# Attention over a KV cache, two blocks: VectorE's copy of the overflow flag ahead of or behind the last sum

## The chip, the cores and the metric

The kernel runs on one core of a Trainium2 chip. The core has five engines, each with its own instruction stream: TensorE (PE, matmuls; PEld are its weight loads), VectorE (DVE), ScalarE (ACT), GpSimd (POOL) and SyncE (SP, which here issues nearly all DMAs). They meet only at semaphores. The metric is the device time of one execution in microseconds (us), lower is better. Before the change it is 738.27 us, the median of three runs (737.86, 738.27 and 738.68).

A profiled execution gives a trace. Its times are counted from the first instruction of the program; the time from there to the last instruction is called the span.

## What is computed

Two independent attention blocks, A and B, with the same shapes. Their results stand side by side in the output.

```python
B, Sq, D = 16, 64, 640
H, Sk, Dh = 32, 512, 128

def block(x, k_cache, v_cache, wq, wo):
    q = (x @ wq).reshape(B, Sq, H, Dh).transpose(0, 2, 1, 3)
    scores = einsum("bhqd,bhkd->bhqk", q, k_cache) * Dh ** -0.5
    o = einsum("bhqk,bhkd->bhqd", softmax(scores), v_cache)
    return o.transpose(0, 2, 1, 3).reshape(B, Sq, H * Dh) @ wo

out = concatenate([block(A...), block(B...)], axis=-1)      # 16 x 64 x 1280, bfloat16
```

All inputs are bfloat16. The two key and two value caches are by far the most of what is read.

## The kernel before

**Tiles and stages.** Two batch entries are handled together, so that 2 x 64 query rows fill 128 partitions. A *pack* is such a pair of batch entries with four heads; there are 128 packs. For each pack the kernel projects the queries (QP), transposes the keys on VectorE (KT), computes the scores (S), takes the exponential on ScalarE (EX), multiplies by the reciprocal of the row sum on GpSimd (NM), transposes the probabilities (TR, copied out by TE), multiplies by the values (PV, copied out by OE) and adds the product with the output weights to PSUM (OP). Four packs make a group, and after a group VectorE adds its part to an accumulator (OS). When the last heads of a block are in, SP stores 128 rows of the output (ST).

**The order of the work.** It is written out by hand. `build_plan` gives every operation a time, in units of packs, from the table `AT` in `Cfg`, and each engine executes its operations sorted by that time. From what each operation reads and writes, the semaphore waits are derived (`order_waits`): a wait that an earlier one on the same engine already covers is dropped. So to change a number in `AT` can change the place of an operation in its engine's order, and the waits with it.

**The exponential is taken without subtracting the maximum.** This holds as long as no row sum is out of bounds. Whether that was so is examined at the end: VectorE reduces all reciprocals to a maximum and a minimum and makes a 0 or 1 for each of 128 partitions (FL1, lines 907 to 916), TensorE multiplies that vector with itself to the number of good partitions (FLM, a matmul of one element, line 919), and VectorE copies the number to SBUF as an integer (FLC, line 923). This integer is the flag. Every engine, at the end of its program, waits for the flag copy, loads the flag into a register (line 987) and branches (line 988): at 128 over the general version of the program, which is in the code but not executed here, and otherwise into it. SP then waits until the output has landed:

```python
def run(e, eng):
    run_program(e, eng, 0)
    e.wait_ge(sems[0][("s_flc_dve",)], 1)
    ...
        e.reg_load(r, flag[0:1, 0:1])
        e.br_eq(r, 128, on_true=over, on_false=again).branch_hint(ahead[eng])
    ...
    if eng == "sp":
        all_done(e, 0, ("d_out",))
```

**The last pack** is done in finer steps, so that the end is short. Its product with the output weights is made in two halves of 320 columns (OPH, line 827), VectorE adds each half to the accumulator (OSH, line 835: the sums of the change), and SP stores each half as soon as its sum is there (STH, line 842). In the table `AT` the first sum stands at 1.75, the flag copy at 1.77 and the second sum at 1.8; the stores stand at 1.85 and 1.9, on SP. On TensorE the flag's matmul (1.68) stands between the matmuls of the first half (1.65) and the second (1.7). Line 529 is that of the block that holds all five programs: to it the trace puts SP's wait for the output and the drains and semaphores that close the program.

Of the kernel before, what the change touches and what calls it, by code (L numbers as in the profile page):

```python
# [20 lines left out]
class Cfg:  # L21
# [16 lines left out]
              RCZ=(0.475, 0.6), NMZ=(0.48, 0.49, 0.61, 0.62), TR=1.293, TE=(1.432, 1.47), PV=1.701, OE=(1.888, 2.013), ZO=2.221,  # L38
              OP=2.387, OS=2.576, LDWO=2.6, ST=2.8,
              TRH=(1.0, 1.05), TEH=(1.15, 1.2), TEX=1.2, PVH=(1.45, 1.46), OEH=(1.5, 1.55), OPY=(1.1, 1.57),  # L40
              OPZ=(1.65, 1.7), OSH=(1.75, 1.8), STH=(1.85, 1.9), FL1=1.3, FLM=1.68, FLC=1.77, WP0=-1.75,
              WP1=(-3.5, -2.55, -2.45, -1.5, -0.5, 0.5, 0.6, 1.5))


# [42 lines left out]
def build_plan(dims, cfg, general):  # L87
# [12 lines left out]
    def add(eng, kind, idx, ts, reads=(), writes=()):  # L100
        op = Op(eng, kind, idx, ts, reads, writes)
        ops.append(op)
        at[(kind, idx)] = op
        return op

    def add_output(n):
# [6 lines left out]
        if n == N - 1:  # L113
            for a in range(2):
# [5 lines left out]
                    [("B", 4), ("B", 5), ("xe", 0)] if a == 0 else [("SB", 2), ("SB", 3), ("xe", 1)])  # L120
                add("pe", "OPH", (n, a), n + AT["OPZ"][a], [("xe", 0), ("xe", 1), ("wo", j)], [("B", 6 + a)])
                add("dve", "OSH", (g, a), n + AT["OSH"][a], [("acc", g % NBP)], [("B", 6 + a), ("out_sb", a)])
# [944 lines left out]
```

## Time and profile before

| | |
|---|---|
| median of three runs | 738.27 us (737.86 to 738.68) |
| the profiled execution's own time | 737.86 us |
| its span, first to last instruction | 736.1 us |
| granted TensorE clock, mean | 0.981 of full speed |
| busy share of the span: PE / PEld / DVE / ACT / POOL | 92% / 72% / 72% / 72% / 57% |
| DMA, mean over the span | 401 GB/s, 295 MB |

Times of the trace are microseconds from the start of the span unless they are marked ns. A line of the timeline has the start, the duration, the engine, the source line, the operation with what it writes and reads, and in brackets how long the engine was idle before and what ended that. The lower-case q behind an engine (SPq, PEldq) is its sequencer: there stand register loads, branches, semaphores and DMA issues, which do not count as busy. "DMA to landing" is the time from a DMA's issue to its last semaphore count. Where DMA packets are listed by queue, q1 carries the kernel's loads and stores, and q8 and q14 carry instructions, that is, program code. Shares of a DMA queue are shares of 16 DMA engines over the stretch asked for.

### The profile page before, as it was taken

How to read it: one execution, taken by the hardware profiler on the slowest of the kernel's cores; microseconds unless marked ns; L12 is line 12 of the kernel's file. 1: busy time of each engine (PE TensorE's matmuls, PEld its weight loads, DVE VectorE, ACT ScalarE, POOL GpSimd, SP SyncE). 2: the span in 40 equal slices, each digit the busy share in tenths (PEclk: the TensorE clock that was granted, in tenths of full speed). 3: DMA queues.
4: the chain of work that ended last, by engine and by line, in shares of the span. 5: the costliest groups of instructions: out<-in, count | busy, mean ns of one | idle time of the engine just before them, and what ended most of it. 6: DMA issues, size and time to landing. Idle time of an engine off the chain costs nothing.

```text
span 736.1 us, 61429 instructions
## 1 busy us (share of the span) xinstructions
PE 679.2 (92%) x28502; PEld 532.5 (72%) x28502; DVE 526.9 (72%) x819; ACT 533.2 (72%) x1574; POOL 416.5 (57%) x596
## 2 busy tenths in 40 slices
PE   3679999999989999999988999999998899999997
PEld 2457877877767777777766787777776678778785
DVE  7347877878767876867756777776676578788884
ACT  1348787877876887777865777777776687878874
POOL 3635656557864555454865565565577456555561
PEclk9889999999999999999998999999999999999999
DMA  8999999999999999999999999999999999999991
GB/s 325 393 392 411 415 415 414 414 416 413 416 400 410 417 417 416 415 419 416 416 412 400 416 414 414 414 414 413 416 416 405 404 418 417 415 419 416 417 400 45
DMA packets 76131, 295.06 MB, mean 401 GB/s; under 512 B 9536, under 2 KB 24512, under 8 KB 59712
## 3 DMA queue, kind: packets, MB, share of 16 engines
q1 hardware_dynamic: 73328, 291.90, 98.4%
q10 hardware_dynamic: 2768, 2.79, 1.2%
q8 instruction: 10, 0.16, 0.1%
q14 instruction: 25, 0.20, 0.1%
HBM read 292.03 MB, written 2.62 MB: 400 GB/s over the span
## 4 chain that ended last, share of the span: by engine, by line
PE 60%; DMA 27%; SPq 5%; DVE 3%; issue 2%; POOL 1%; ACT 0%; ACTq 0%
PE ps L863 14%; PE ps L883 13%; PE ps L684 12%; PE ps L708 12%; DMA wo_sb<-in_B_wo_dram 8%; PE ps L770 7%; DMA kn_ring<-in_B_k_cache_dram 5%; DMA kn_ring<-in_A_k_cache_dram 5%; DMA xn_ring<-in_B_x_dram 5%; SPq L631 3%; SPq L642 2%; DMA ws_sb<-in_A_wq_dram 2%; DMA wo_sb<-in_A_wo_dram 2%; DVE kt_ring L698 1%; DVE pT_sb L850 1%
## 5 line engine op out<-in xcount | busy, mean ns | idle before, releaser
L758 POOL TENSOR_SCALAR pn_ring<-pn_ring,recip 128x512 bf16<-128x512 bf16 x508 | 342.1, 692 | 244.9 <-DVE recip L750 238.5
L698 DVE STREAM_TRANSPOSE kt_ring<-kn_ring 128x1024 f32<-128x1024 f32 x256 | 302.4, 1220 | 65.9 <-DMA kn_ring<-in_B_k_cache_dram 35.7
L737 ACT ACTIVATE pn_ring<-ps 128x512 bf16<-128x512 f32 x512 | 296.4, 592 | 6.8 <-PE ps L708 6.8
L850 DVE COPY pT_sb<-ps 128x1024 bf16<-128x1024 bf16 x256 | 170.3, 676 | 103.5 <-PE ps L770 80.1
L863 PE MATMUL ps<-pT_sb,v_ring 32*128 32x64 bf16 x16448 | 162.1, 193 | 25.3 <-DVE pT_sb L850 12.7
L863 PEld LDWEIGHTS ps<-pT_sb,v_ring 32*128 32x128 bf16 x16448 | 147.5, 92 | 39.2 <-issue 28.7
L684 PE MATMUL ps<-xT_ring,wqp_sb 128*128 128x128 bf16 x2560 | 166.3, 221 | 7.5 <-POOL xT_ring L673 7.5
L684 PEld LDWEIGHTS ps<-xT_ring,wqp_sb 128*128 128x128 bf16 x2560 | 158.0, 114 | 14.0 <-issue 7.8
L883 PE MATMUL ps<-wo_sb,oT_sb 128*128 128x320 bf16 x1024 | 165.3, 305 | 0.0
L871 ACT ACTIVATE oT_sb<-ps 128x256 bf16<-128x256 f32 x257 | 84.7, 381 | 109.3 <-PE ps L863 109.3
L708 PE MATMUL ps<-kt_ring,qs_ring 32*64 32x512 bf16 x4096 | 140.6, 386 | 3.6 <-issue 3.6
L690 ACT ACTIVATE qs_ring<-ps 128x512 bf16<-128x512 f32 x128 | 76.4, 597 | 65.3 <-PE ps L684 62.6
L883 PEld LDWEIGHTS ps<-wo_sb,oT_sb 128*128 128x128 bf16 x1024 | 91.0, 99 | 37.9
L770 PEld LDWEIGHTS ps<-ident,pn_ring 64*128 64x128 bf16 x4096 | 68.8, 96 | 66.9 <-ACT oT_sb L871 48.0
L737 ACT ACTIVATION_READ_ACCUMULATOR pn_ring<-ps 128x1 f32 x512 | 105.3, 206 | 0.0
L770 PE MATMUL ps<-ident,pn_ring 64*128 64x64 bf16 x4096 | 83.8, 192 | 12.3 <-POOL pn_ring L758 4.5
L708 PEld LDWEIGHTS ps<-kt_ring,qs_ring 32*64 32x64 bf16 x4096 | 53.2, 104 | 33.2 <-issue 5.9
L750 DVE RECIPROCAL recip<-rowsum 128x2 f32<-128x2 f32 x256 | 41.0, 160 | 30.3 <-ACT pn_ring L737 24.6
L875 ACT ACTIVATE ps<-zeros 128x256 f32<-128x256 bf16 x128 | 49.5, 387 | 4.1
L652 POOL COPY wqp_sb<-ws_sb 128x1280 bf16<-128x1280 bf16 x32 | 39.5, 1253 | 18.3 <-DMA ws_sb<-in_A_wq_dram 15.1
L664 ACT ACTIVATE xe_sb<-ps 128x640 bf16<-128x640 bf16 x32 | 23.0, 717 | 3.6 <-PE ps L658 3.6
L673 POOL COPY xT_ring<-xe_sb 128x640 bf16<-128x640 bf16 x16 | 11.5, 716 | 21.9 <-PE ps L770 21.9
(42 smaller groups left out, 103.7 us busy)
## 6 DMA issues: line engine op xcount, KB each, us to landing
v_ring<-in_A_v_cache_dram SPq DMA_DIRECT2D x128, 512.0 KB, 12.9
kn_ring<-in_B_k_cache_dram SPq DMA_DIRECT2D x128, 512.0 KB, 14.0
v_ring<-in_B_v_cache_dram SPq DMA_DIRECT2D x128, 512.0 KB, 12.8
kn_ring<-in_A_k_cache_dram SPq DMA_DIRECT2D x112, 512.0 KB, 14.1
kn_ring<-in_A_k_cache_dram SPq DMA_DIRECT2D x32, 256.0 KB, 9.0
wo_sb<-in_A_wo_dram SPq DMA_DIRECT2D x8, 640.0 KB, 14.6
ws_sb<-in_B_wq_dram SPq DMA_DIRECT2D x10, 512.0 KB, 17.3
wo_sb<-in_B_wo_dram SPq DMA_DIRECT2D x8, 640.0 KB, 15.0
```

Source lines behind the costliest of these rows:

```text
L684: last = e.matmul(ps[:, 1, f * 128:(f + 1) * 128], w[:, kt, f, :], xT_ring[:, xs, kt, :], start=(kt == 0), stop=(kt == KT - 1))
L690: ins = e.activation(qs_ring[:, op.idx % NQ].rearrange("p f b q -> p (f b q)"), ps[:, 1, :], ACTF.Copy, scale=scale)
L698: ins = e.transpose(dst.rearrange("p c b (h l) -> p c h b l", h=8, l=2), src)
L708: last = e.matmul(ps[64 * b:64 * b + 64, i, :], qs_ring[rows, n % NQ, f, b, :], kt_ring[rows, n % NKT, :, f // 2, b, :, f % 2], start=(f = ...
L737: ins = e.activation(dst, src, ACTF.Exp, scale=1.0, accum_out=sum_of(h))
L758: ins = e.tensor_scalar(pn_view(h), pn_view(h), recip[:, h:h + 1], 1.0, ALU.mult, ALU.mult)
L770: last = e.transpose(pt_bank(b)[:, 64 * c:64 * c + 64], pn[rows, c, :], ident[rows, rows], tile_position=(64 * b, 0))
L850: ins = e.tensor_copy(pT_sb[:, b].rearrange("p t q -> p (t q)"), pt_bank(b))
L863: last = e.matmul(ps[:, 4 + i, 64 * b:64 * b + 64], v_ring[rows, n % NV, b, c, :], pT_sb[rows, b, c, :], start=(t == 0 and i < 2), stop=(t ...
L871: ins = e.activation(oT_sb[:, 2 * a:2 * a + 2, :], o_ps[:, 2 * a:2 * a + 2, :], ACTF.Copy)
L875: ins = e.activation(z_ps, zeros[:, :].unsqueeze(2).broadcast_to([128, 2, 128]), ACTF.Copy)
L883: last = e.matmul(out_ps[:, s, :], oT_sb[:, i, :], wo_sb[:, 4 * j + i, s * NH0:(s + 1) * NH0], start=(j == 0 and i == 0), stop=(j == NJ - ...
```

## The change

The flag copy's time in the table goes from 1.77 to 1.82. The second sum stands at 1.8, so on VectorE the order "first sum, flag copy, second sum" becomes "first sum, second sum, flag copy". No operation is added or removed, and the order on the other engines is as it was.

```diff
               TRH=(1.0, 1.05), TEH=(1.15, 1.2), TEX=1.2, PVH=(1.45, 1.46), OEH=(1.5, 1.55), OPY=(1.1, 1.57),
-              OPZ=(1.65, 1.7), OSH=(1.75, 1.8), STH=(1.85, 1.9), FL1=1.3, FLM=1.68, FLC=1.77, WP0=-1.75,
+              OPZ=(1.65, 1.7), OSH=(1.75, 1.8), STH=(1.85, 1.9), FL1=1.3, FLM=1.68, FLC=1.82, WP0=-1.75,
               WP1=(-3.5, -2.55, -2.45, -1.5, -0.5, 0.5, 0.6, 1.5))
```

## The prediction

> **What bounds the kernel now.** I read the page first. The chain of waits is 60% TensorE and 27% DMA; the slices of the span show 400 to 419 GB/s in nearly every slice between the first and the last, which hold 325 and 45. The change touches none of that: it moves one VectorE instruction in the last 5 us, so I read the tail alone: the timeline from 726 us, the flag's readers (the rows of line 987), what follows them (lines 988 and 529), SP's waits, and the DMA packets after 732 us.
>
> The timeline (start, duration) of the order that is changed:
>
> ```profile
> 730.76 0.16 PE L919 MATMUL ps<-good 128*1 128x1 bf16 x1
> 730.86 0.72 PE L827 MATMUL ps<-wo_sb,xe_sb 128*128 128x320 bf16 x4
> 730.94 0.49 DVE L835 TENSOR_TENSOR out_sb<-acc,ps 128x320 bf16<-128x320 f32 x1 [1.48 <-PE ps L827]
> 731.34 0.14 DVE L923 CAST flag<-ps 1x1 int32<-1x1 f32 x1
> 731.46 1.01 SPq L842 DMA_DIRECT2D out_dram<-out_sb  x2
> 731.61 0.49 DVE L835 TENSOR_TENSOR out_sb<-acc,ps 128x320 bf16<-128x320 f32 x1
> ```
>
> The flag copy (line 923) sits between the two sums (line 835). TensorE's last matmuls end at 730.86 + 0.72 = 731.58, and the second sum starts at 731.61: it waits for TensorE, not for the flag copy, which ended at 731.48. SP's second store is issued at 732.13.
>
> The flag's readers, their branches, the end of each engine's work, and what SP waits for:
>
> ```profile
> L987 PEldq TENSOR_LOAD <-flag x1: 486/486/486, 731.5 to 731.5; - x1
> L987 DVEq TENSOR_LOAD <-flag x1: 544/544/544, 731.6 to 731.6; - x1
> L987 SPq TENSOR_LOAD <-flag x1: 507/507/507, 732.5 to 732.5; - x1
> L988 ACTq COMPARE_BRANCH  x1: 68/68/68, 732.0 to 732.0; - x1
> L988 DVEq COMPARE_BRANCH  x1: 84/84/84, 732.2 to 732.2; - x1
> L529 ACTq DRAIN  x1: 64/64/64, 732.5 to 732.5; - x1
> L529 DVEq DRAIN  x1: 52/52/52, 732.8 to 732.8; - x1
> L529 SPq COMPARE_BRANCH  x1: 53/53/53, 735.7 to 735.7; - x1
> SPq L529 <- DMA out_dram<-out_sb: 2.6, 1, 2.6
> DMA to landing us min/median/max: 1.6/2.6/3.6
> ```
>
> ScalarE, GpSimd, TensorE and VectorE read the flag as soon as it is there, branch at 732.0 to 732.2 and are drained by 732.9. SP branches at 733.1, and then waits 2.6 us, until 735.7, for the output to land; the span ends 0.4 us later. So the second store sets the end. The last row is strange: of two stores of the same size the first took 1.6 us from issue to landing, the second 3.6.
>
> Why 3.6? The packets, first of 732.1 to 732.85, then of 732.85 to 733.5, then of 733.5 to 734.2:
>
> ```profile
> DMA packets 144, 0.08 MB, mean 109 GB/s; under 512 B 16, under 2 KB 144, under 8 KB 144
> ...
> DMA packets 129, 0.10 MB, mean 148 GB/s; under 512 B 14, under 2 KB 126, under 8 KB 126
> ...
> q1 hardware_dynamic: 126, 0.07, 35.2%
> q14 instruction: 3, 0.02, 16.3%
> ...
> DMA packets 16, 0.03 MB, mean 36 GB/s; under 512 B 1, under 2 KB 15, under 8 KB 15
> ...
> q1 hardware_dynamic: 15, 0.01, 9.6%
> q8 instruction: 1, 0.02, 8.8%
> ```
>
> A store is 144 packets (128 rows of 640 bytes and 16 below 512 B): nine for each of 16 DMA engines if shared evenly. The first store's 144 ran in one piece. Of the second, 126 = 14 x 9 ran in one piece and were over by about 733.4; the other 18, two engines' share, ran between 733.66 and 734.72. In between stand code fetches: three packets of 8 KB from the queue q14, starting by the peaks of the GB/s line at about 733.09, 733.16 and 733.4, then one of 16 KB from q8 at about 733.93. Shares give the durations: 0.163 x 16 x 0.65 us / 3 = 0.57 us for a q14 packet here, and 0.986 us for the q8 one. A store packet took 0.352 x 16 x 0.65 / 126 = 29 ns in the clear and 0.096 x 16 x 0.70 / 15 = 72 ns beside the 16 KB fetch. So two DMA engines held back their part of the last store for code that the engines fetch after their branches. Branch to packet: ScalarE's 732.0 to 733.09, VectorE's 732.2 to 733.4, some 1.1 to 1.2 us each. That the branch triggers the fetch is my inference from order and distance; no row names the owner.
>
> **The change part by part.** *Removed from between the sums:* one cast of 0.14 us. It lay in the wait for TensorE (731.48 to 731.58), so the second sum gains nothing: TensorE's end holds it at 731.61. Bounds: 0 and -0.02 us ("issue" between 731.59 and 731.61); I take 0. If TensorE were earlier the cast would have cost up to 0.14.
>
> *Added behind the second sum:* the same cast. Its spacing behind a sum is 731.34 - 730.94 = 0.40 us, so it starts at 731.61 + 0.40 = 732.01 and ends at 732.15: the flag is 0.67 us later. Its own wait, for the one-by-one matmul, was over at 730.92, and the second sum's wait for TensorE's later matmuls covers it. Behind it on VectorE stands only VectorE's own load of the flag. SP's two stores wait for the sums, not for the flag, and SP's queue is past both before it looks at the flag: its load starts at 732.5, 0.35 us after the new flag. SP: 0.
>
> *Moved by it:* the flag loads of TensorE, ScalarE, GpSimd and VectorE with their branches and drains. The first three move by 0.67 us; VectorE's load, now issued at 731.6, by 0.55 to 0.67. VectorE's drain comes at about 733.5, and SP ends its second wait at 733.7 at the earliest: hidden by 0.2 us at least against SP's drain. If SP were that early the cover is thin, but it holds.
>
> *Code fetches:* they move with the branches, from 733.09, 733.16, 733.4 and 733.93 to about 733.76, 733.83, 734.0 and 734.6. The second store's packets do not move (issue 732.13) and in the clear are over by 733.4, as 14 of 16 engines show. So the first fetch comes 0.35 us after the last store packet, where now it comes among the first. The second store then lands as the first did: 732.13 + 1.6 = 733.7 rather than 735.7. Bounds of this term: -2.0 us (like the first store) and 0 (like the second now); I take -2.0, since the geometry is then that of the first store, with no fetch among its packets.
>
> *What is late next:* behind 733.7 come SP's drain and the closing semaphores, 0.4 us now and the same then; the four other engines are drained by 733.5.
>
> Sum: 0 + 0 - 2.0 = -2.0 us. The profiled execution took 737.86 us, 736.1 of them span and 1.8 around it; it becomes 735.9, span 734.1. It is the fastest of the three runs shown, 0.4 us below their median of 738.27, to which I apply the same difference: 736.3.
>
> **The rivals.** *Code comes too late.* The fetched code may be needed. Now the 16 KB fetch ends at 734.92, 1.2 us before the end of the span, so any need for it is hidden. After the change it would run from 734.6 to 735.6, behind an end at 734.1. If the code after the closing semaphores (or the branch) lies in it, up to 735.6 - 734.1 = 1.5 us come back: 736.3 to 737.8, most likely 737.2. For it: something is fetched, by every engine. Against it: ScalarE's drain runs 0.4 us after its branch, 0.6 us before the first q14 packet, so the branch's target was there. [...]
>
> *The fetches are not the cause, or do not move.* If the two engines are slow for another reason, or fetches start by a clock of their own, the store lands at 735.7 as now: 738.3. If the collision keeps its shape and rides along with the flag, 738.27 + 0.67 = 738.9. Against: the first store, without fetches, was not slow, and the 18 packets are exactly two engines' worth.
>
> *Slower: the store still falls behind the fetches, which now bunch.* SP's own fetch (8 KB, at 734.43, 0.31 us long by its share of 2.4% of 0.8 us) stands alone today; beside the 16 KB one at 734.6 it would hold a late engine longer. Then the last store packet goes out 0.67 + 0.31 us later: 738.27 + 0.98 = 739.3. It decides only if the second store's packets on these engines are not out by 733.76, 0.35 us later than the 14 others; to pass 0.2% a further half microsecond of fetch is needed.
>
> **How the numbers follow.** 0.2% of 738.27, about what a measurement of this kernel can tell from no change, is 1.48 us: faster is below 736.8, slower above 739.75. The forecast gets 0.64: 735.7 to 736.8 with the scatter of the runs (0.4 either way), nearly all of it faster (0.61). Late code gets 0.20: a quarter below 736.8 (0.05), the rest the same (0.15). Unmoved or riding collision: 0.10, the same. The slower rival: 0.06, most of it over the bound (0.05) if a second fetch joins. So faster 0.66, same 0.29 with a remainder of the forecast and of the slower rival, slower 0.05. The range takes the forecast and the late code: 735.6 to 738.0.
>
> **What would show it.** Right: line 923 at about 732.0, behind both sums; flag loads of four engines at 732.2, branches at 732.7 to 732.9; 144 store packets in one piece before 733.4; both stores landing in 1.6 us; SP's wait for the output 0.6 instead of 2.6; span near 734.1. Wrong: a late group of store packets on some engines again; fetches still at 733.1; a second sum later than 731.61; or a span of 734.1 with the total not following, which would be the late code.

## The result and the profile after

The changed kernel takes 735.56 us, the median of 17 runs (734.64 to 737.14); the kernel before, run beside it, 737.69 us (17 runs with the three shown earlier, 736.62 to 741.35). The ratio is 0.9969 with a 95% interval of 0.9960 to 0.9978: faster by 0.3%, or 2.3 us (1.6 to 3.0). The profiled execution took 736.13 us with a span of 734.4 us (before 737.86 and 736.1).

The end of the changed kernel's timeline (start, duration, engine, line):

```profile
731.21 0.49 DVE L835 TENSOR_TENSOR out_sb<-acc,ps 128x320 bf16<-128x320 f32 x1 [1.69 <-PE ps L827]
731.89 0.49 DVE L835 TENSOR_TENSOR out_sb<-acc,ps 128x320 bf16<-128x320 f32 x1 [0.18 <-PE ps L827]
732.29 0.14 DVE L923 CAST flag<-ps 1x1 int32<-1x1 f32 x1
```

Everything stands 0.28 us later than before, since the body of the kernel ended later in this execution; so I count from the start of the second sum (731.61 before, 731.89 now). The two sums are as far apart as before (0.67 and 0.68 us). The flag copy now starts 0.40 us behind the second sum. It started 0.27 us ahead of it. From the second sum to the end of the span it was 736.1 - 731.61 = 4.5 us, and is 734.4 - 731.89 = 2.5 us: 2.0 us less.

Where they went stands in the row of SP's wait for the output and in the landing of the two stores. SP's waits of the changed kernel:

```profile
SPq L529 <- DMA out_dram<-out_sb: 0.6, 1, 0.6
```

The rows of the stores (line 842), the last being issue to landing, least, median and most:

```profile
L842 SPq DMA_DIRECT2D out_dram<-out_sb x2: 332/344/356, 731.7 to 732.4; - x2
...
DMA to landing us min/median/max: 1.6/1.6/1.6
```

The wait is 0.6 where it was 2.6, and both stores land in 1.6 us where the second took 3.6. The DMA packets from 733.1 to 733.75 us and from 733.75 to 735 us:

```profile
DMA packets 144, 0.08 MB, mean 126 GB/s; under 512 B 16, under 2 KB 144, under 8 KB 144
...
q14 instruction: 4, 0.03, 9.1%
q8 instruction: 1, 0.02, 5.8%
```

All 144 packets of the second store run in one piece, and the code fetches come behind them. The late packets were not all of the 2.0 us: the last packet ends 2.6 us behind the issue before (734.72 - 732.13) and 1.2 us now (733.62 - 732.40), which is 1.4 us; from the last packet to the landing it was 1.0 us and is 0.4. What fills the other 0.6 us is not in the trace. The rows of the branches (line 988) say when the engines branch:

```profile
L988 ACTq COMPARE_BRANCH  x1: 68/68/68, 733.0 to 733.0; - x1
L988 POOLq COMPARE_BRANCH  x1: 65/65/65, 733.0 to 733.0; - x1
```

Counted from the second sum that is 1.1 us, where it was 0.4: the 0.67 us by which the flag moved.

### The profile page after: what moved, and what is told of

It reads as the page before. It is cut to its first block, busy times and chain, and to the rows that moved or that the text cites. A ratio compares the mean times of both kernels' runs of the same rounds, so it can differ in the third digit from the quotient of the medians.

```text
span 734.4 us, 61429 instructions
## 1 busy us (share of the span) xinstructions
PE 680.7 (93%) x28502; PEld 533.7 (73%) x28502; DVE 527.0 (72%) x819; ACT 532.9 (73%) x1574; POOL 416.5 (57%) x596
## 4 chain that ended last, share of the span: by engine, by line
PE 61%; DMA 27%; SPq 5%; DVE 3%; issue 2%; POOL 1%; ACT 0%; ACTq 0%
PE ps L863 14%; PE ps L883 13%; PE ps L684 12%; PE ps L708 12%; PE ps L770 7%; DMA wo_sb<-in_B_wo_dram 6%; DMA kn_ring<-in_B_k_cache_dram 5%; DMA xn_ring<-in_B_x_dram 5%; DMA kn_ring<-in_A_k_cache_dram 5%; DMA wo_sb<-in_A_wo_dram 4%; SPq L631 3%; DMA ws_sb<-in_A_wq_dram 2%; SPq L642 2%; DVE kt_ring L698 1%; DVE pT_sb L850 1%
## 5 line engine op out<-in xcount | busy, mean ns | idle before, releaser
L673 POOL COPY xT_ring<-xs_sb 128x640 bf16<-128x640 bf16 x16 | 11.5, 716 | 21.8 <-PE ps L770 21.8
```

## The experiments

The theory: after its branch an engine fetches code, a fetch that comes ahead of the second store holds one DMA engine's share of that store, and SP waits for the last share. By it, what costs is the time of the branches, not the place of the copy on VectorE. A share is nine packets, since 126 packets in one piece and 18 late in before, and 135 and 9 in wait_act, are multiples of nine. That the nine belong to one of 16 DMA engines is an inference from these counts: the trace does not name the DMA engine of a packet, nor the engine that a code fetch is for. The load of the flag goes with its branch (some 0.5 us ahead of it) in every experiment, so "the branch" below means the two together. The table gives each run's time against the kernel before; the time from the start of the second sum to the end of the span; SP's wait for the output; and how many of the second store's 144 packets come late, that is, behind a gap or behind a code fetch. The last three are from one profiled execution each.

| run | ratio to before (95%) | second sum to end, us | SP's wait, us | late packets |
|---|---|---|---|---|
| before | 1 | 4.5 | 2.6 | 18 |
| the change | 0.9969 (0.9960 to 0.9978) | 2.5 | 0.6 | 0 |
| wait_all | 0.9964 (0.9951 to 0.9978) | 2.5 | 0.6 | 0 |
| no_branch | 0.9979 (0.9970 to 0.9988) | 2.5 | 1.2 | 0 |
| wait_act_pool | 0.9972 (0.9958 to 0.9985) | 2.5 | 0.6 | 0 |
| wait_act | one execution | 3.6 | 1.7 | 9 |
| wait_pool | one execution | 3.5 | 1.6 | 9 |
| wait_pe | 0.9996 (0.9984 to 1.0008) | 4.2 | 2.2 | 18 |
| late_store | 0.9984 (0.9972 to 0.9995) | 3.0 | 0.6 | 0 |
| late_store3 | 1.0008 (0.9995 to 1.0020) | 5.3 | 2.3 | 27 |
| flag_later | 0.9997 (0.9987 to 1.0007) | 3.8 | (the flag) | 0 |
| matmul_last | 0.9975 (0.9959 to 0.9992) | 2.5 | 0.6 | 0 |

### Only the branches later, the copy where it was

```diff
 # before, in run()
             e.wait_ge(sems[0][("s_flc_dve",)], 1)
+            if eng in ("pe", "act", "dve", "pool"):
+                e.wait_ge(sems[0][("s_osh_dve",)], 2)
```

> Before's order on VectorE (flag copy between the two sums), but TensorE, ScalarE, GpSimd and VectorE also wait for the second sum before they load the flag, so that only their branches come later (by some 0.6 us). Theory (code fetches behind the branches hold the second store on two DMA engines): the store's packets run in one piece, it lands in about 1.6 us instead of 3.6, the span is 1.7 to 2.0 us shorter, ratio to before about 0.997, as with the change. Rival (what costs is the cast's place between the sums on VectorE): the second store still takes about 3.6 us and the time is that of before, ratio 1.000.

The ratio is 0.9964. VectorE's order is that of before, as its timeline shows:

```profile
729.74 0.49 DVE L835 TENSOR_TENSOR out_sb<-acc,ps 128x320 bf16<-128x320 f32 x1 [1.54 <-PE ps L827]
730.15 0.14 DVE L923 CAST flag<-ps 1x1 int32<-1x1 f32 x1
730.42 0.49 DVE L835 TENSOR_TENSOR out_sb<-acc,ps 128x320 bf16<-128x320 f32 x1
```

and yet SP's wait for the output is 0.6 us, and the span ends at 732.9, 2.5 us behind the second sum. So the copy's place between the sums cost nothing; all of the gain that the trace shows comes from the later branches.

### No branches

```diff
 # before, in run()
             run_program(e, eng, 0)
-            e.wait_ge(sems[0][("s_flc_dve",)], 1)
-            ...                                     # load of the flag, branch, general version
             if eng == "sp":
                 all_done(e, 0, ("d_out",))
```

> Before's order, the flag is made but nobody loads it or branches on it, and the general version of the program is left out of the code; so the fallback for row sums out of bounds is left out. Theory: without the four branches there is no bunch of code fetches within the second store; it lands in about 1.6 us; ratio about 0.997, no better than the change by more than 0.3 us, since the flag's path does not set the end there. Rival (cast's place): 3.6 us and ratio 1.000. If the flag's loads and branches cost on their own, the ratio is below 0.996.

The mark for the branch's hint, 300 operations ahead, is gone too, and the trace has no code fetch that starts behind the first sum. The second store lands in 1.6 us, and the ratio is 0.9979. The end is no closer to the second sum than with the change: the flag's path, once out of the store's way, costs nothing more. SP's wait is longer, 1.2 us, because SP gets to it earlier: 1.6 - 1.2 = 0.4 us behind the issue of the second store, against 1.6 - 0.6 = 1.0 with the change.

### Which engine's branch

The same edit as in the first experiment, for some engines only:

```diff
+            if eng in ("act", "pool"):      # wait_act_pool; ("act",), ("pool",) and ("pe",) in the others
+                e.wait_ge(sems[0][("s_osh_dve",)], 2)
```

> Before's order; of the four engines only ScalarE and GpSimd wait for the second sum before they load the flag, so two of the 8 KB fetches move by some 0.6 us; TensorE's 16 KB fetch and VectorE's 8 KB fetch stay. Theory with ScalarE's and GpSimd's fetches as those that hold the store: the packets run in one piece, landing 1.6 us, 2.5 us from the start of the second sum to the end of the span (before 4.5). If TensorE's fetch is the cause: nearly as before, 4.0 us or more.

> Before's order; only ScalarE waits for the second sum before it loads the flag, GpSimd's branch stays early. If each of the two engines' fetches holds one DMA engine's share of the store: 9 of the 144 packets come late instead of 18, and the landing takes between 1.6 and 3.6 us (about 2.4 us, the landing of the first of the two late shares in before). If ScalarE's fetch alone is the cause: none late, 1.6 us. If GpSimd's alone: 18 late, 3.6 us.

> The counterpart: only GpSimd waits for the second sum, ScalarE's branch stays early. If each fetch holds one DMA engine's share: 9 of 144 packets late, landing between 1.6 and 3.6 us. If GpSimd's fetch alone is the cause: none late, 1.6 us. If ScalarE's alone: 18 late, 3.6 us.

> Before's order; only TensorE waits for the second sum before it loads the flag, so the 16 KB fetch moves by some 0.6 us and the 8 KB fetches stay. Theory: 18 packets still start late, behind the 8 KB fetches, but are not slowed by the 16 KB one: landing 2.0 to 2.7 us, 2.9 to 3.6 us from the start of the second sum to the end of the span (before 4.5). If TensorE's fetch is the whole cause: 2.5 us. If it has no part: 4.5 us.

With ScalarE and GpSimd both late the whole gain is there. With one of them late, half. The packets of wait_act from 733.5 to 734.1 us, and from 734.1 to 735 us:

```profile
q1 hardware_dynamic: 135, 0.08, 40.9%
q8 instruction: 1, 0.02, 12.1%
q14 instruction: 2, 0.02, 10.3%
...
q14 instruction: 2, 0.02, 5.9%
q1 hardware_dynamic: 9, 0.01, 2.4%
```

and of wait_pool from 731.2 to 731.8 us, and from 731.8 to 733 us:

```profile
q1 hardware_dynamic: 135, 0.08, 40.9%
q14 instruction: 2, 0.02, 12.6%
...
q1 hardware_dynamic: 9, 0.01, 2.2%
```

135 packets in one piece are 15 shares of nine, and nine come late: with one of the two engines still early one share is held, whichever of the two it is. One held share costs 1.0 to 1.1 us, two cost 2.0 in before and, as the next paragraph has it, 1.7 in wait_pe.

wait_pe missed its expectation: 4.2 us to the end, not 2.9 to 3.6, and a ratio that can't be told from 1. The reason is that it did not test what it should. TensorE's branch came 0.7 us later, but the 16 KB fetch, which I take for TensorE's, started 733.75 - 731.32 = 2.43 us behind the second sum, against 733.93 - 731.61 = 2.32 before. It did start earlier, at 733.55 - 731.80 = 1.75 us, where the two 8 KB fetches had moved away (wait_act_pool). Counted from TensorE's own branch the packet starts 1.23 to 1.30 us later in every profile but two: in before it is 1.87 us and in wait_pool 2.09. So in before it came some 0.6 us late itself (1.87 less 1.23 to 1.30); behind what, no run tells, and neither how much of the 2.0 us is owed to it. The 18 late packets stand among the fetches as before.

### The store later, into the fetches

The changed kernel, with the second sum repeated behind the flag copy (once, and twice), and the store waiting for that. The function that makes the sum again is left out here:

```diff
 # after, in add_output(), last pack
+                if a:                                       # late_store3: two of these
+                    add("dve", "OSR", (g, a), n + 1.83, [("acc", g % NBP)], [("B", 6 + a), ("out_sb", a)])
                 loads.append((n + AT["STH"][a], 5,
                               add("sp", "STH", (g, a), n + AT["STH"][a], [("out_sb", a)], [("out_dram", g, a)])))
```

> The changed order, with the second sum made a second time behind the flag copy and the second store waiting for that: the flag and the code fetches stay, the store is issued about 0.55 us later, so its packets fall among the fetches again. Theory: two DMA engines are late again, landing 2.5 to 3.6 us after the issue instead of 1.6, so the end comes 1.5 to 2.6 us after that of the changed kernel, about the time of before or up to 0.5 us over it. Rival (a store that is merely later): landing stays 1.6 us, the end comes 0.55 us later than in the changed kernel, ratio to before about 0.998.

This fell on the rival's side. The end came 0.5 us later than with the change, no more; the packets of 732.7 to 733.3 us:

```profile
q1 hardware_dynamic: 144, 0.08, 43.5%
q14 instruction: 3, 0.02, 14.8%
q8 instruction: 1, 0.02, 11.1%
```

No packet was held, but the store hardly met the fetches either. Packet by packet, its 144 run from 732.77 to 733.15 us; two of the four fetches in this stretch start in the last 0.1 us of that (733.05 and 733.11), and two behind it (733.27 and 733.28). What this run does show comes from a comparison: the first fetch starts 733.052 - 732.767 = 0.285 us behind the store's first packet here and 733.922 - 733.615 = 0.307 us in wait_act, yet wait_act has a held share. So what decides is not when the fetch's data start. One repetition more:

> The changed order with the second sum made three times in all, so that the second store is issued about 1.5 us after the start of the second sum (changed kernel 0.52, late_store 1.04). The first code fetch should start some 2.15 us after the start of the second sum, as in those two, and the store's packets 2.4 us after it: behind the fetch, where in late_store they started 0.23 us ahead of it. Theory (a DMA engine that has begun a code fetch holds its share of the store): 18 packets come late, the landing takes 2.3 us or more instead of 1.6, and from the start of the second sum to the end of the span it is 4.0 to 5.1 us. Rival (merely later): landing 1.6 us, 3.5 us to the end of the span.

The store's issue came 1.0 us later than with the change by the expectation's count, and the end 2.8 us later (5.3 against 2.5). SP's waits and the packets from 734.68 to 736.9 us:

```profile
SPq L533 <- DMA out_dram<-out_sb: 2.3, 1, 2.3
```

```profile
DMA packets 22, 0.03 MB, mean 12 GB/s; under 512 B 3, under 2 KB 20, under 8 KB 20
...
q1 hardware_dynamic: 20, 0.01, 3.9%
```

20 packets late in this stretch (of the table's 27, the first seven lie ahead of it) are more than two shares, and three of them are the short ones, of which each share has one: a third engine was held as well. So the stall came back with the changed order of VectorE, and the time went back to that of before (1.0008, not to be told from 1). It was larger than expected (5.3, not 4.0 to 5.1), by the third share: the other two are over at 735.16, and the third runs from 735.67 to 736.21.

The trace keeps the start, length and queue of every DMA packet, though not its DMA engine. Read one by one, the packets show where a held share starts, in all five profiles that have one:

| run | code fetch in front, its end (us) | first packet of the held share (us) |
|---|---|---|
| before | 8 KB, 733.677; 8 KB, 733.824 | 733.673; 733.820 |
| wait_act | 8 KB, 734.380 | 734.377 |
| wait_pool | 8 KB, 732.124 | 732.120 |
| wait_pe | 8 KB, 733.506; 8 KB, 733.533 | 733.503; 733.530 |
| late_store3 | 8 KB, 734.525; 8 KB, 734.656; 16 KB, 735.672 | 734.522; 734.653; 735.667 |

Each of the nine held shares starts 3 to 5 ns ahead of the end of a fetch packet. The packets of one share follow each other in the same way: the first two that come late in before are 733.673 to 733.705 and 733.702 to 733.734. From these 3 to 5 ns I infer that each held share stood right behind a code fetch on its DMA engine, which no row names. The third one of late_store3 starts at the end of the 16 KB packet, which I take for TensorE's by its distance from that branch (1.25 us).

What tells late_store from the others is the order of branch and issue. Its branches and those of late_store3 (rows of the branch's line, which the added lines have moved down):

```profile
L993 ACTq COMPARE_BRANCH  x1: 68/68/68, 732.0 to 732.0; - x1
L993 POOLq COMPARE_BRANCH  x1: 65/65/65, 732.0 to 732.0; - x1
```

```profile
L998 ACTq COMPARE_BRANCH  x1: 68/68/68, 732.9 to 732.9; - x1
L998 POOLq COMPARE_BRANCH  x1: 65/65/65, 732.9 to 732.9; - x1
L998 PEldq COMPARE_BRANCH  x1: 479/479/479, 733.0 to 733.0; - x1
```

late_store issues its second store at 731.93, just ahead of both branches: none held. late_store3 issues at 733.40, behind three branches: three held. Before: branches at 732.0 and 732.1, issue at 732.13: two held. wait_act: GpSimd's at 732.7, issue at 732.78, ScalarE's at 733.4: one held. wait_pool: ScalarE's at 730.4, issue at 730.50, GpSimd's at 731.1: one held. In wait_pe two branches (731.7 and 731.8) precede the issue (731.83), two are held. For ScalarE and GpSimd the count of branches ahead of the issue is the count of held shares behind 8 KB packets in all eleven profiles that have branches, and a tenth of a microsecond is enough: GpSimd's branch began 0.08 us ahead of the issue in before (held) and 0.08 us behind it in late_store (not held). TensorE's branch counts in late_store3, where it began 0.43 us ahead of the issue. It does not in before, wait_act, wait_pool and wait_act_pool, where it began 0.05 or 0.06 us ahead and no share starts at the end of a 16 KB packet; why is left open.

### The flag much later

```diff
 # after, in em_FLC(), in short: three reductions into a spare tile ahead of the copy
+            first = e.tensor_reduce(spare[:, 0:1], recip[:, :], AX.X, ALU.max)
+            e.tensor_reduce(spare[:, 1:2], recip[:, :], AX.X, ALU.max)
+            e.tensor_reduce(spare[:, 2:3], recip[:, :], AX.X, ALU.max)
             ins = e.tensor_copy(flag[:, :], ps[0:1, 0, 0:1])
```

> The changed order with three more reductions of 0.68 us each ahead of the flag copy: the flag comes 2.0 us later still. Theory: the store lands as in the changed kernel (1.6 us); the flag's path now ends last: VectorE's drain moves from 733.7 to 735.7, 1.5 us behind SP's drain of the changed kernel, so the time is 1.5 us over the changed kernel's, ratio to before about 0.999. The rival that the code behind the end waits for the fetched pages: more than that, 2.0 us or more over the changed kernel, since the fetches move by the whole 2.0 us.

The copy came 1.8 us later than with the change (733.19 - 731.00 = 2.19 us behind the second sum, against 0.40), the reductions being 0.6 us apart and not 0.68. The end came 1.3 us later (3.8 against 2.5). Now SP itself waits for the flag:

```profile
SPq L991 <- DVE flag L927: 1.5, 1, 1.5
```

The rival that the fetched code is needed fell. There is no instruction packet between 732.3 us and the end of the span at 734.8 us: all 144 packets there are the store's, so no fetch that goes with the branches had begun when the span ended. The execution took 736.55 us, 1.75 more than its span. Before it was 1.76, where the fetches were over more than a microsecond ahead of the end; with the change 1.73. So neither the span nor the time around it shows anything that waited for that code. By the ratios the cost is 0.9997 - 0.9969 = 0.28%, 2.1 us, which taken alone would suit the rival; but the two intervals leave it anywhere between 0.09% and 0.47%, so the times do not decide here, and the trace does.

### A little further

```diff
-  FLM=1.68, FLC=1.82          # the changed kernel
+  FLM=1.72, FLC=1.82          # the flag's matmul behind TensorE's last matmuls
```

> The changed kernel with the flag's one-element matmul behind TensorE's last matmuls instead of between them (its time in the table 1.72 instead of 1.68). The flag copy stands behind the second sum and should not wait for it. TensorE's last matmuls, and so the second sum, come about 0.1 us earlier after the first sum: 3.1 us from the start of the first sum to the end of the span, where the changed kernel has 3.18. Too little for the time to show: ratio to before that of the changed kernel, 0.997. If the flag comes later by it, the fetches move away from the store, which costs nothing until VectorE's drain ends last (0.5 us later).

VectorE's timeline shows the two sums back to back:

```profile
731.09 0.96 DVE L835 TENSOR_TENSOR out_sb<-acc,ps 128x320 bf16<-128x320 f32 x2 [1.49 <-PE ps L827]
731.97 0.14 DVE L923 CAST flag<-ps 1x1 int32<-1x1 f32 x1
```

From the first sum to the end of the span it is 734.1 - 731.09 = 3.0 us, against 734.4 - 731.21 = 3.2 with the change. The time can't show it: 0.9975 (0.9959 to 0.9992) is not to be told from 0.9969. It is the shortest end of all the versions, but no version was shown to be faster than the change.

## Why the prediction was right or wrong

**The stated time and range were wrong; the mechanism and its size held.** 735.56 us lies 0.04 us under the range's low end of 735.6, and 0.7 us under the forecast of 736.3. The step that failed is the last of the sum, "to which I apply the same difference", and with it the scatter of "0.4 either way" behind the range, whose low end lay only 0.7 us under the forecast (736.3 less 0.4 would even be 735.9). Both took three runs, with their median of 738.27, for the kernel's own median and scatter. Over 17 runs that is 737.69, and in three later comparisons 736.89, 737.51 and 737.16 (27, 26 and 13 runs). Of the miss of 0.7 us, 738.27 - 737.69 = 0.6 is this base; 0.1 is the effect, 2.13 us between the medians against 2.0. The scatter had to be taken wider: single runs of before range from 735.7 to 741.4. The two parts of a time, span and what lies around it, tell where it comes from: the latter is 1.68 to 1.79 us in all 27 runs of before in the first set of experiments, so the scatter is in the span. Much of it comes from the body, ahead of all that the change touches: in the profiles the second sum starts anywhere from 729.99 us (wait_pool) to 732.27 us (wait_act).

**The term of -2.0 us** was right: 4.5 to 2.5 us in the trace, landing 3.6 to 1.6, wait 2.6 to 0.6. Its cause, code fetches that hold two of 16 shares, was an inference then; wait_all, no_branch and the two single-engine runs now bear it out: a held share starts 3 to 5 ns ahead of the end of a fetch packet, and it goes with the branch that is moved (18 late packets in before, 9 in wait_act and wait_pool, none in wait_act_pool). That the two stood on one DMA engine stays an inference. Whether the branch itself or the load of the flag ahead of it asks for the code was not separated, and 0.6 of the 2.0 us lies behind the last packet, where the cause is open.

**The cast's place at nothing** was right: wait_all leaves it between the sums and has the whole gain. **The shift of 0.67 us** was right: the branches stand 1.1 us behind the second sum instead of 0.4. **The drains** stayed hidden: VectorE's started at 733.7, SP's at 734.2.

**The fetches** moved as forecast only in part. The first 8 KB one started at 734.04, which is the forecast 733.76 and the 0.28 us by which everything was later. The 16 KB one was to come at 734.6 + 0.28 = 734.88 and came at 734.25, 2.36 us behind the second sum against 2.32 before: its late start in before was taken for its distance from the branch. It did no harm, because the store was out by 733.62.

**The margin was misread.** I took the 0.35 us between the last store packet and the first fetch's data to be what decides. By late_store and wait_act, with fetches that start 0.285 and 0.307 us behind the store's first packet, what goes with a held share is a branch ahead of the store's issue, and there the change has 733.0 - 732.4 = 0.6 us in hand. So the forecast was right on this point by a margin other than the one it gave. The rule is read off eleven profiles; no run was made to test it.

**The rivals.** Late code: refuted by flag_later. Nor did a fetch hold up any of the four branches: the drains behind them start at 733.45 to 733.66 in the changed kernel, 0.5 to 0.6 us behind their branches and ahead of the first fetch at 734.04, and at 732.50 to 732.81 in before, ahead of the first at 733.09. What code is fetched no row shows. A collision that does not move or rides along: refuted by the packets in one piece. The bunched fetches of the slower rival came about, all five between 734.0 and 734.5, but behind the store, where they cost nothing; late_store3, which puts the store behind the branches, is what that rival would have looked like, at 1.0008.

## What to carry to other kernels

At the end of this kernel the last store's landing is the path, and a branch of ScalarE or GpSimd ahead of the store's issue went with nine packets of it behind a code fetch, 1.0 to 1.1 us for one such share and 1.7 to 2.0 for two. In another kernel, look at how many of a store's packets run late, and whether they come in whole shares (nine of 144 here). Branches can be held back until the last store is issued; here the same 2 us came from moving the copy and from a wait ahead of the flag's load. A forecast in absolute time needs a base with more than three runs, or a range that takes in the scatter of the base.

## What was not expected

A tenth of a microsecond in the order of a branch and a DMA issue goes with a whole microsecond or two of landing time: the branches came at 732.03 and 732.05 and the issue at 732.13 in before (landing 3.6 us), at 731.99 and 732.01 with the issue at 731.93 in late_store (1.6 us from the issue until SP goes on). And a held share waits longer than the fetch's own data lasts: in wait_act the store's first packet starts at 733.62 us, and the held share at 734.38, 0.76 us later, behind a fetch whose data began only at 733.92 and lasted 0.46 us. What kept the share waiting from about 733.62 to 733.92 is not in the trace.
